# An attention and two feed-forward layers on one core: k loaded ahead of q, and the first sequence's v scaled with its second group of blocks

## Chip, core and metric

The kernel runs on one core of a Trainium2 chip. The metric is device time in microseconds (us) for one whole execution. Three runs of the kernel before gave 715.36, 717.83 and 713.94 us; their median is 715.36 us. The engines are named as the profile names them: PE multiplies matrices, PEld loads its weights, DVE and ACT work on vectors, POOL does small setup work and indirect transfers, SP issues most transfers ("SPq" in a row is its queue of issues).

## What is computed

```
scores = where(block_i >= block_j, q @ k.T / 8, -1e9)     # 4 x 8 heads, 576 rows of 64, blocks of 64
attn   = exp(scores - rowmax); attn /= rowsum + 1e-9
x      = attn @ v                                          # 2304 tokens x 512
x      = elu(x @ w_in) @ w_out                             # 512 -> 2048 -> 512
# then, for tokens with x @ w_skip > 0: the best of 8 experts
e      = argmax(x @ w_gate);  x += gate * (relu(x @ w1[e]) @ w2[e])
```

All of it must come out in f32 accuracy. Much of the kernel therefore multiplies f16 pairs (a high half and the rest, "halves"), and halves need a scale that is found from the size of the data.

## The kernel before

**Attention.** The work is cut into units (sequence b, pair of heads p, block i of 64 queries). A sequence has nine blocks in groups: blocks 0 to 3, then 4 to 7 (with 8 apart in the first sequence). A unit is a score product `s` (PE), a row maximum `mx` (DVE), `e = exp` with its row sum `su` (ACT), the division into `en` or `ehl` (ACT, and DVE for the low half), a transpose into `et`, and, for a whole group, the product `xps` with v (PE), copied into `xt` (ACT). The first sequence is special: q and k come as f32 in a layout that needs no transpose. Blocks 0 to 3 (the first group, needed by the first 256 tokens) use v in f32 straight from the load (`vx`) and `en` in f32, turned on PE (`tp`) and copied to `et` on ACT or DVE. Only its second group uses v's halves (`vt`, made in `prep_v`), which need v's scale: `vflat` loads all of v of one sequence, `vmax` squares and sums it on ACT (the tile `vflat`), and `vscale` brings the sum to all partitions with two small matmuls (`bm1`, `bm2`, tile `bm`) and some DVE steps on `col`.

**First layer.** It goes through nine chunks of 256 tokens. For each, eight products `h = xt @ w_in` of 256 hidden units each, ELU into `g`, and eight products `y += g @ w_out`. The first two chunks use the weights in f32 (`twi`, `two`). The weights arrive as 64-bit values (`rw`), and DVE makes f32 of each half tile with one TENSOR_SCALAR and two SCALAR_TENSOR_TENSOR steps (`conv`, 32 pieces). `h` has two PSUM buffers, `y` two (shared with `bm` and other small products), `s` three. `post` reads `y` into `pay`.

**What sets the order.** Nothing is issued while the program is described. A recorder keeps each step with the tiles it reads and writes, a cost, and its number in the description. `order()` then fills the engines in simulated time: among the steps that are ready on an engine, the one with the lowest number goes first. The description order is thus a priority, and a step that is described later gives way to others. Steps of one engine run strictly in the order so found. The description is given by `A`, `pre`, `post_` and `ex`, lists by position: position x holds the scores of unit x, exponentials of unit x - 1, and so on. `addex(x, ...)` appends steps to position x. The first sequence's first group is positions 0 to 15 and its second group begins at position 16. The first chunk's `h` is described after position 20. SP's transfers are issued one after another, and a transfer that must wait holds up those behind it. Steps in `hot` and the loads at the start have a base of -300, ahead of all others.

**Lines that the change touches.** `load_q0` (two transfers a block, one for each half of the partitions; PE takes it as loaded), `load_k0` (one transfer a block; `prep_k` then scales it by 1/8 on ACT before PE may use it), the `addex` list over b, and the start of the description behind `VF`. All recorded steps have line 320 in the profile, so tiles name them.

Of the kernel before, what the change touches and what calls it, by code (L numbers as in the profile page):

```python
# [357 lines left out]
def tile_kernel(ctx, tc, q, k, v, w_in, w_out, w_skip, w_gate, w1, w2, q0, k0, out):  # L358
# [43 lines left out]
    def newcol(n=1):  # L402
        c = ncol[0]
        ncol[0] += n
        return slice(c, c + n)

    def cf(s):
        return col[:, s]
# [7 lines left out]
    def bc_max(src):  # L416
        p1 = misc([1, 128], "bm1")
        rc.tensor.transpose(out=p1, in_=src, identity=ident)
        t1 = sm.tile([1, 1], BF16, tag="bmt", bufs=2, name="bmt")
        rc.vector.tensor_reduce(out=t1, in_=p1, axis=AX.X, op=ALU.max)  # L420
        p2 = misc([128, 1], "bm2")
        rc.tensor.matmul(out=p2, lhsT=ones16[0:1, :], rhs=t1, start=True, stop=True)
        return p2
# [112 lines left out]
    def scale_bits(T_, S_, I_):  # L536

        Ti = T_.bitcast(I32)
        rc.vector.tensor_scalar(out=Ti, in0=Ti, scalar1=24, scalar2=None, op0=ALU.logical_shift_right)
        rc.vector.tensor_scalar(out=S_.bitcast(I32), in0=Ti, scalar1=-B23, scalar2=204 * B23, op0=ALU.mult, op1=ALU.add)  # L540
        rc.vector.tensor_scalar(out=I_.bitcast(I32), in0=Ti, scalar1=B23, scalar2=50 * B23, op0=ALU.mult, op1=ALU.add)
# [78 lines left out]
    def vflat(b):  # L620
        t = ap.tile([128, H * S * D // 128], F32, tag="kt1", bufs=1, name="vflat")
        rc.sync.dma_start(out=t, in_=v[b].rearrange("s h d -> (s h d)").rearrange("(p x) -> p x", p=128))
        st["vf", b] = t

    def vmax(b):
        if "vmx" not in st:
            st["vmx"] = newcol(4)
        s = st["vmx"].start
        t = st.pop(("vf", b))
        rc.scalar.activation(out=t, in_=t, func=AF.Square, accum_out=col[:, s + b:s + b + 1])  # L630

    def vscale(i):
        s = st["vmx"].start
        if i == 0:
            src = col[:, s:s + 1]
        else:
            c = newcol()
            rc.vector.tensor_reduce(out=cf(c), in_=col[:, s:s + B], axis=AX.X, op=ALU.max)
            src = cf(c)
        T_, S_, I_, P_ = (cf(newcol()) for _ in range(4))  # L640
        rc.vector.tensor_copy(T_, bc_max(src))
        scale_bits(T_, S_, I_)
        rc.vector.tensor_scalar(out=P_, in0=I_, scalar1=2.0 ** 14, scalar2=None, op0=ALU.mult)
        st["v", i] = S_, P_
        if i == 0:
            c = cf(newcol())
            rc.vector.tensor_scalar(out=c, in0=st["v", 0][1], scalar1=2.0 ** -28, scalar2=None, op0=ALU.mult)
            st["x0"] = c
        if i == 1:
            c = cf(newcol())  # L650
            rc.vector.tensor_tensor(out=c, in0=st["v", 0][1], in1=st["v", 1][0], op=ALU.mult)
            c2 = cf(newcol())
            rc.vector.tensor_scalar(out=c2, in0=c, scalar1=2.0 ** -28, scalar2=None, op0=ALU.mult)
            st["mix"] = c2
# [6 lines left out]
    def trows(n):  # L661
        return 128 if n < 4 else 64

    def load_raw(nm, b, n):
        if b == 0 and nm != "v":
            (load_q0 if nm == "q" else load_k0)(n)
            return
        src = {"q": q, "k": k, "v": v}[nm]
        r = trows(n)
        t = ap.tile([128, H, D], F32, tag="raw", bufs=5, name="raw")  # L670
        rc.sync.dma_start(out=t[0:r], in_=src[b, n * 128:n * 128 + r])
        RAW[nm, b, n] = t
# [17 lines left out]
    def load_q0(n):  # L690

        r = trows(n)
        x = QT[0, n] = ap.tile([128, 2, 4, r], F32, tag="qt" if n < 4 else "qh", bufs=3 if n < 4 else 1, name="qx")
        for h in range(2):
            (rc.gpsimd if n > 1 else nc.vector).memset(x[64 - 64 * h:128 - 64 * h, h], 0.0)
        for h in range(2):
            rows = slice(64 * h, 64 * h + 64)
            rc.sync.dma_start(out=x[rows, h].rearrange("p a t -> p (a t)"), in_=q0[rows, 512 * n:512 * n + 4 * r])

    def k0_of(n):  # L700
        return KT[0][:, 512 * n:512 * n + 4 * trows(n)]

    def load_k0(n):

        if n == 0:
            KT[0] = ap.tile([128, 4 * S], F32, tag="kt0", bufs=1, name="kx")
        rc.sync.dma_start(out=k0_of(n), in_=k0[:, 512 * n:512 * n + 4 * trows(n)])

    def load_v0():

        x = X0["v"] = ap.tile([128, 2, H, D], F32, tag="ehl", bufs=2, name="vx")
        for n in range(2):
            rc.sync.dma_start(out=x[:, n].rearrange("p h d -> p (h d)"), in_=v[0, 128 * n:128 * n + 128].rearrange("p h d -> p (h d)"))
            RAW["v", 0, n] = x[:, n]
# [552 lines left out]
    ex = [[] for _ in A]  # L1267

    def addex(x, *fns):
        ex[x].extend(fns)  # L1270

    def L(nm, b, n):
        return lambda: load_raw(nm, b, n)

    def P(f, b, n):
        return lambda: f(b, n)

    for b in range(B):
        g0, g1 = ubase[b, 0], ubase[b, 1]
        if b:  # L1280
            addex(g0 + 1, L("v", b, 1))
        addex(g0 + 1, L("k", b, 2), L("q", b, 2))
        if b:
            addex(g0 + 5, P(prep_v, b, 1))
        addex(g0 + 4, P(prep_k, b, 2), P(prep_q, b, 2), L("v", b, 2), L("k", b, 4))
        addex(g0 + 7, P(prep_v, b, 2), P(prep_k, b, 4), L("q", b, 4), L("v", b, 4))
        addex(g0 + 10, P(prep_q, b, 4), P(prep_v, b, 4), L("k", b, 3), L("v", b, 3), L("q", b, 3))
        addex(g0 + 13, P(prep_k, b, 3), P(prep_v, b, 3))
        addex(g0 + 14, P(prep_q, b, 3))
        if b + 1 < B:  # L1290
            addex(g1 + 8, L("k", b + 1, 0), L("q", b + 1, 0))
            addex(g1 + 11, P(prep_k, b + 1, 0), P(prep_q, b + 1, 0), L("v", b + 1, 0), L("k", b + 1, 1))
            addex(g1 + 14, P(prep_v, b + 1, 0), P(prep_k, b + 1, 1), L("q", b + 1, 1))
            addex(g1 + 18, P(prep_q, b + 1, 1))
# [67 lines left out]

    VF = [4, 5, 6, 6, 7, 8, 9]
    rc.base = -300
    load_q0(0)
    load_k0(0)
    load_q0(1)
    load_k0(1)
    load_v0()
    setup_consts()  # L1370
    for x0, x1, y in ((0, 64, -2048.0), (64, 128, 0.0), (128, 192, 4096.0)):
# [3 lines left out]
    rc.base = 0  # L1375
    load_to(8)
    vflat(0)
    ex[6][0:0] = [lambda: vmax(0), lambda: vscale(0)]
    addex(9, P(prep_v, 0, 0), P(prep_v, 0, 1))
    for x in range(6):  # L1380
        on_a(4 + 2 * x, conv_step)
    for x in range(8):
# [636 lines left out]
```

## Time and profile before

| | us |
|---|---|
| median of three runs | 715.36 |
| lowest, highest | 713.94, 717.83 |
| profiled execution, its own time | 716.24 |
| its span (first to last instruction) | 714.5 |
| PE busy | 678.7 (95%) |
| DVE busy | 568.6 (80%) |
| ACT busy | 504.5 (71%) |
| mean granted PE clock | 0.983 |

The profiled execution's own time has 1.7 us outside its span, and it is 0.88 us above the median. PE is the busiest engine; in the page's 40 slices it is at 9 tenths or more nearly everywhere except the first three slices and the last two. A busy PE can still run at half its clock, which the page gives by slice.

### The profile page before, as it was taken

To read this page: it belongs to the slowest core of one execution; us is meant where nothing else is said; L and a number is where in the kernel's file an instruction comes from. 1 tells how busy PE (TensorE), PEld (TensorE's weight loads), DVE (VectorE), ACT (ScalarE), POOL (GpSimd) and SP (SyncE) were. 2 spreads that over 40 slices of the span, in tenths; PEclk is the share of its full clock that TensorE was granted. 3 is DMA by queue.
4 is the path that set the end of the run, shared out by engine and by line. 5 is a ranking of instruction groups with operands and counts; after the bars stand their busy time and mean duration, and the time that the engine had idled before them with its cause. 6 is when DMAs were issued, how large, how long until landed. Compare 5 with 4: busy or idle time off the path is not lost. (4 is left out here: it accounts for less than half of the span.)

```text
span 714.5 us, 17462 instructions
## 1 busy us (share of the span) xinstructions
PE 678.7 (95%) x6553; PEld 464.8 (65%) x6553; DVE 568.6 (80%) x1640; ACT 504.5 (71%) x1081; POOL 81.9 (11%) x124
## 2 busy tenths in 40 slices
PE   6799998999999999999999999999999999999894
PEld 4478445774576666667656658667576777687683
DVE  5899978988999989988779946999687645666452
ACT  5866478999886878878578736865466548697582
POOL 2000000020001000100100100100105034313012
PEclk9799999999999999999999999999999999999897
DMA  8989999974978788998278159536264779989531
GB/s 281 331 283 377 255 217 202 168 171 88 193 159 137 161 185 216 188 191 176 59 120 176 21 101 337 224 97 200 60 218 132 208 180 240 198 267 207 171 120 17
DMA packets 205882, 130.96 MB, mean 183 GB/s; under 512 B 170699, under 2 KB 171861, under 8 KB 205264
## 3 DMA queue, kind: packets, MB, share of 16 engines
q1 hardware_dynamic: 200736, 120.84, 67.2%
q0 software_dynamic: 3952, 6.70, 4.8%
q10 hardware_dynamic: 1088, 2.10, 0.9%
q8 instruction: 56, 0.92, 0.5%
q14 instruction: 50, 0.41, 0.2%
HBM read 73.59 MB, written 12.75 MB: 121 GB/s over the span
## 5 line engine op out<-in xcount | busy, mean ns | idle before, releaser
L320 PE MATMUL h<-xt,win 128*128 128x256 f16 x1344 | 157.5, 273 | 1.5 <-DVE n L320 1.0
L320 PE MATMUL y<-wout,g 128*128 128x512 f16 x672 | 155.7, 379 | 0.0
L320 PEld LDWEIGHTS <-win 128*128 128x128 f16 x1344 | 128.9, 98 | 23.4 <-issue 1.3
L320 PEld LDWEIGHTS <-g 128*128 128x128 f16 x672 | 63.9, 98 | 66.7 <-issue 0.4
L320 ACT ACTIVATE e<-s,mx 128x512 f32<-128x512 f32 (+4 forms) x160 | 82.1, 516 | 19.6 <-DVE ehl L320 9.2
L320 DVE TENSOR_REDUCE mx<-s 128x1 f32<-128x512 f32 (+4 forms) x160 | 75.3, 477 | 16.6 <-PE s L320 16.0
L320 ACT ACTIVATE ehl<-e,su 128x512 f16<-128x512 f32 (+4 forms) x144 | 74.1, 561 | 12.9 <-DMA et<-ehl 4.0
L320 DVE SCALAR_TENSOR_TENSOR ehl<-e,su,ehl 128x512 f16<-128x512 f32 (+4 forms) x144 | 75.8, 552 | 6.0 <-ACT ehl L320 5.8
L320 PE MATMUL y<-two,g 128*128 128x512 f32 x128 | 59.9, 604 | 0.0
L320 PE MATMUL h<-xt,twi 128*128 128x256 f32 x256 | 59.2, 384 | 0.3 <-DVE g L320 0.3
L320 ACT ACTIVATE g<-el,col 128x512 f16<-128x512 f32 x56 | 40.2, 718 | 21.6 <-DVE el L320 21.3
L320 ACT ACTIVATE el<-h,col 128x512 f32<-128x512 f32 x56 | 38.2, 682 | 24.1 <-PE h L320 22.8
L320 PEld LDWEIGHTS <-p 128*128 128x128 f16 x984 | 46.8, 99 | 9.1 <-PEq L1853 4.1
L320 PEld LDWEIGHTS h<-xt,twi 128*128 128x128 f32 x256 | 47.3, 190 | 7.9 <-issue 1.0
L320 PEld LDWEIGHTS <-vt 128*64 128x64 f16 x1368 | 35.4, 111 | 22.8 <-issue 15.7
L320 PE MATMUL s<-kt,qt 128*64 128x512 f16 (+5 forms) x288 | 48.7, 298 | 0.7 <-ACT e L320 0.5
L320 PE MATMUL xps<-et,vt 128*64 128x128 f16 (+1 forms) x1368 | 44.1, 213 | 3.9 <-DMA et<-ehl 2.2
L320 DVE SCALAR_TENSOR_TENSOR g<-el,col,g 128x512 f16<-128x512 f32 x56 | 41.7, 745 | 3.3 <-ACT g L320 3.0
L320 DVE SCALAR_TENSOR_TENSOR el<-h,col,el 128x512 f32<-128x512 f32 x56 | 41.8, 746 | 1.4
L1554 DVE SCALAR_TENSOR_TENSOR p<-p,n,p 128x1024 f16<-128x1024 f32 x32 | 40.6, 1281 | 2.7 <-ACT p L1553 2.6
L320 PE MATMUL s<-kx,qx 128*128 128x128 f32 (+5 forms) x96 | 34.7, 523 | 7.6 <-ACT kx L320 6.7
L320 POOL DMA_INDIRECT lst_d<-li,si x16 | 19.3, 1209 | 188.5 <-DVE li L320 90.6
(237 smaller groups left out, 1161.7 us busy)
## 6 DMA issues: line engine op xcount, KB each, us to landing
p<-in_moe_w_dram SPq DMA_DIRECT2D x45, 512.0 KB, 5.7
rw<-in_moe_w_in_dram SPq DMA_DIRECT2D x16, 512.0 KB, 8.4
rw<-in_moe_w_out_dram SPq DMA_DIRECT2D x16, 512.0 KB, 7.9
pb<-in_moe_w_dram SPq DMA_DIRECT2D x10, 512.0 KB, 4.9
vflat<-in_v_dram SPq DMA_DIRECT2D x4, 1152.0 KB, 8.9
out_dram<-pay SPq DMA_DIRECT2D x18, 256.0 KB, 3.3
pay_d<-pay SPq DMA_DIRECT2D x18, 256.0 KB, 3.7
raw<-in_v_dram SPq DMA_DIRECT2D x14, 256.0 KB, 3.0
```

The source lines that it names most:

```text
L320: rec.call(e, time, lambda: getattr(self.real, op)(*args, **kw), reads, writes, dma)
L1554: rc.call("dve", 1.2, lambda: nc.vector.scalar_tensor_tensor(out=half(1), in0=raw.t, scalar=sc, in1=half(0), op0=ALU.mult, op1=ALU.subtrac ...
```

## The change

The description changes in two ways, for the first sequence only. At the start, for each of the first two blocks of 128 rows, the transfer of k is issued before the two of q. And v's largest value (`vmax`), its scale (`vscale`) and the five `prep_v` are described at positions 14 to 18, where they stood at positions 6 to 13.

```diff
-        addex(g0 + 7, P(prep_v, b, 2), P(prep_k, b, 4), L("q", b, 4), L("v", b, 4))
-        addex(g0 + 10, P(prep_q, b, 4), P(prep_v, b, 4), L("k", b, 3), L("v", b, 3), L("q", b, 3))
-        addex(g0 + 13, P(prep_k, b, 3), P(prep_v, b, 3))
+        addex(g0 + (7 if b else 17), P(prep_v, b, 2))
+        addex(g0 + 7, P(prep_k, b, 4), L("q", b, 4), L("v", b, 4))
+        addex(g0 + (10 if b else 18), P(prep_v, b, 4))
+        addex(g0 + 10, P(prep_q, b, 4), L("k", b, 3), L("v", b, 3), L("q", b, 3))
+        addex(g0 + 13, P(prep_k, b, 3))
+        addex(g0 + (13 if b else 18), P(prep_v, b, 3))
...
-    load_q0(0)
-    load_k0(0)
-    load_q0(1)
-    load_k0(1)
+    for n in range(2):
+        load_k0(n)
+        load_q0(n)
...
-    ex[6][0:0] = [lambda: vmax(0), lambda: vscale(0)]
-    addex(9, P(prep_v, 0, 0), P(prep_v, 0, 1))
+    addex(14, lambda: vmax(0))
+    addex(15, lambda: vscale(0))
+    addex(16, P(prep_v, 0, 0), P(prep_v, 0, 1))
```

The recorder makes a new order from this. The engines' orders differ from the start through the first three sequences' attention and agree word for word from about 357 us of the trace before to the end. Three places follow.

DVE ahead of the first `h`, before. `mx` are row maxima of the second group's scores, `bmt` is a step of v's scale, `twi` is weight conversion, and `et_263` is the last transposed block that the first chunk needs.

```order
L320 TENSOR_REDUCE mx_255<-s_256 128x1
L320 TENSOR_REDUCE bmt_188<-bm1_187 1x1
L320 SCALAR_TENSOR_TENSOR twi4_280<-rw_146,twi4_280 128x512
L320 TENSOR_SCALAR twi4_280<-rw_147 128x512
L320 COPY et_263<-tp_264 128x512
```

The same place now; `et_261` is the tile that was `et_263`.

```order
L320 TENSOR_REDUCE mx_252<-s_253 128x1
L320 SCALAR_TENSOR_TENSOR twi3_277<-rw_153,twi3_277 128x512
L320 COPY et_261<-tp_262 128x512
L320 SCALAR_TENSOR_TENSOR twi3_277<-rw_153,twi3_277 128x512
L320 TENSOR_REDUCE bmt_242<-bm1_241 1x1
```

The copy of `et` has moved ahead of the scale's `bmt`, with one conversion step ahead of it where two were. On PE the scale's second product `bm2` now stands behind the last product with `et` and ahead of the score product that precedes `h`, and the two score products `s_245` and `s_253` stand next to each other, where a product `xps` stood between them.

SP around the first transposing transfer of the second group, before.

```order
L320 DMA rw_152<-in_moe_w_in_dram 128x2x512
L320 DMA rw_153<-in_moe_w_in_dram 128x2x512
L320 DMA rw_143<-in_moe_w_out_dram 128x1024
L320 DMA_TRANSPOSE et_273<-ehl_267 128x12x128
L320 DMA rw_147<-in_moe_w_out_dram 128x1024
```

The same place now.

```order
L320 DMA rw_152<-in_moe_w_in_dram 128x2x512
L320 DMA_TRANSPOSE et_273<-ehl_267 128x12x128
L320 DMA rw_153<-in_moe_w_in_dram 128x2x512
L320 DMA rw_143<-in_moe_w_out_dram 128x1024
L320 DMA rw_147<-in_moe_w_out_dram 128x1024
```

The transpose, which waits for DVE's `ehl_267`, has moved ahead of the last load of `w_in` and the first of `w_out`.

ACT at the end of the first chunk, before. `pay_413` and `pay_416` are the chunk's two halves read out of PSUM.

```order
L320 ACTIVATE pay_413<-y_302 128x512
L320 ACTIVATE e32_408,su_407<-s_397,mx_396 128x512
L320 ACTIVATE ehl_406<-e32_401,su_400 128x4x128
L320 ACTIVATE ehl_406<-e32_402,su_400 128x64
L320 ACTIVATE e32_409,su_407<-s_398,mx_396 128x64
L320 ACTIVATE pay_413<-pay_413,rts_414 128x512
L320 ACTIVATE pay_416<-y_303 128x512
```

The same place now.

```order
L320 ACTIVATE pay_413<-y_302 128x512
L320 ACTIVATE e32_402,su_400<-s_391,mx_389 128x64
L320 ACTIVATE sq_418,col_77<-twi7_289 128x1024
L320 ACTIVATE pay_416<-y_303 128x512
L320 ACTIVATE ehl_406<-e32_401,su_400 128x4x128
```

The second readout has moved ahead of the attention's steps.

## Rows read from the trace of the kernel before

**Rows 1.** Engines by stretch: us, busy us (instructions), granted PE clock, DMA share, GB/s.

```profile
0.00:38.10 38.10, 26.44 (x132) 16.64 (x132) 27.19 (x86) 25.24 (x73) 6.59 (x44) 0.87 0.95 303
38.10:100.00 61.90, 61.90 (x275) 40.09 (x273) 59.04 (x124) 37.91 (x71) 0.00 (x0) 1.00 0.94 293
100.00:357.00 257.00, 250.51 (x2467) 165.63 (x2466) 230.06 (x742) 212.41 (x527) 15.37 (x23) 1.00 0.82 165
```

**Rows 2.** Timeline of PE around the first h: start, length, engine, step, [idle before <-releaser].

```profile
30.44 1.62 PE L320 MATMUL s<-kx,qx 128*128 128x384 f32 x2 [0.43 <-issue]
...
32.04 0.70 PE L320 MATMUL xps<-et,vx 128*64 128x128 f32 x4
32.67 1.65 PE L320 MATMUL s<-kx,qx 128*128 128x384 f32 x2
...
36.73 0.66 PE L320 MATMUL xps<-et,vx 128*64 128x128 f32 x8 [1.37 <-DVE et L320]
37.32 0.91 PE L320 MATMUL s<-kx,qx 128*128 128x384 f32 x2
...
38.10 5.43 PE L320 MATMUL h<-xt,twi 128*128 128x256 f32 x24
...
47.70 20.97 PE L320 MATMUL h<-xt,twi 128*128 128x256 f32 x96
```

**Rows 3.** Timeline of the start: SP's issues, ACT's scaling of k, PE.

```profile
0.81 1.22 SPq L320 DMA_DIRECT2D qx<-in_q_dram  x2
...
2.08 0.59 SPq L320 DMA_DIRECT2D kx<-in_k_dram  x1
...
5.51 0.63 ACT L320 ACTIVATE kx<-kx 128x512 f32<-128x512 f32 x1 [3.42 <-DMA kx<-in_k_dram]
...
6.19 0.79 PE L320 MATMUL s<-kx,qx 128*128 128x128 f32 x2 [6.19 <-ACT kx L320]
...
7.52 0.63 ACT L320 ACTIVATE kx<-kx 128x512 f32<-128x512 f32 x1 [1.38 <-DMA kx<-in_k_dram]
```

**Rows 4.** Tile qx up to 45 us: from issue to landing of its ten transfers.

```profile
DMA to landing us min/median/max: 3.4/3.7/10.8
```

**Rows 5.** Timeline of DVE ahead of the first h.

```profile
34.40 0.56 DVE L320 TENSOR_REDUCE mx<-s 128x1 f32<-128x384 f32 x1 [1.10 <-PE s L320]
34.88 0.27 DVE L320 TENSOR_REDUCE bmt<-bm 1x1 bf16<-1x128 f32 x1
35.07 0.67 DVE L320 SCALAR_TENSOR_TENSOR twi<-rw,twi 128x512 int32<-128x512 int32 x1
35.67 0.41 DVE L320 TENSOR_SCALAR twi<-rw 128x512 int32<-128x512 int32 x1
36.01 0.67 DVE L320 COPY et<-tp 128x512 f32<-128x512 f32 x1
```

**Rows 6.** Timeline of ACT: the square of the first sequence's v.

```profile
30.24 2.12 ACT L320 ACTIVATE vflat<-vflat 128x2304 f32<-128x2304 f32 x1
```

**Rows 7.** Timeline of ACT, PE and DVE at the first chunk's end.

```profile
115.04 0.58 ACT L320 ACTIVATE pay<-y 128x512 f32<-128x512 f32 x1
...
115.67 0.16 PE L320 MATMUL bm<-bmt,ones 1*128 1x1 bf16 x1 [1.44 <-ACT pay L320]
...
116.11 0.66 DVE L320 TENSOR_REDUCE rts<-pay 128x1 f32<-128x512 f32 x1
```

**Rows 8.** Engines in two stretches ahead of the first h; columns as in rows 1.

```profile
24.60:28.00 3.40, 1.83 (x18) 1.03 (x16) 3.14 (x9) 2.55 (x7) 0.00 (x0) 1.00 1.06 320
28.00:35.20 7.20, 6.51 (x25) 3.54 (x26) 5.47 (x14) 7.01 (x17) 0.36 (x1) 0.53 1.06 305
```

**Rows 9.** Timeline of SP's transpose, and DVE's last piece of w_in.

```profile
44.82 1.57 SPq L320 DMA_TRANSPOSE et<-ehl  x1
...
54.01 0.42 DVE L320 TENSOR_SCALAR twi<-rw 128x512 int32<-128x512 int32 x1
```

**Rows 10.** Tile rw up to 45 us: from issue to landing of its 17 transfers.

```profile
DMA to landing us min/median/max: 7.2/8.4/10.6
```

## The prediction

> **What bounds the kernel now.** I read the table of engines by stretch first. From 38.1 us, where the first `h` product starts, to 100 us PE is busy for all 61.90 us; from 100 to 357 us it is busy for 250.51 of 257 [rows 1]. Before 38.1 us it is busy for 26.44, part of that at half clock: the mean granted clock there is 0.87 [rows 1]. So PE bounds all but the start, and the start is bound by a chain of small steps on four engines that ends when `xt` is complete and `h` can begin. Work that leaves that chain brings `h` forward, and the rest of the program follows, as long as PE stays fed. PE has the same products to do ahead of `h` as before (three score products of the second group among them), so what counts is the moment at which `h` begins, and any new wait after it.
>
> The timeline of PE around that moment comes next [rows 2]: a 1.37 us wait for DVE's `et`, then the last `xps`, one score product, and `h` at 38.10. The timeline of DVE says why `et` was late: after the row maximum at 34.40 come `bmt` (0.27), two conversion steps, and only at 36.01 the copy [rows 5]. At the other end of the chain PE first starts at 6.19 us, on ACT's scaled k [rows 3].
>
> **The change part by part.** Term A, k ahead of q. No instruction is added; the same three issues a block change places. PE needs scaled k and raw q. Before, SP issues q's two transfers from 0.81 on (1.22 us) and k at 2.08; k has landed by 5.51, ACT scales it for 0.63, and PE starts at 6.19 [rows 3]. Now k goes at 0.81 and, at the shortest landing of such a transfer, 3.4 us [rows 4], is scaled by 0.81 + 3.4 + 0.7 = 4.9, and the last of q is issued at about 0.81 + 0.59 + 0.61 = 2.0, which lands between 5.4 (3.4 us) and 5.7 (3.7 us) [rows 4]. So q ends the wait in place of k and the 0.63 us of scaling no longer stands behind the last landing: PE starts at about 5.5, a gain of 0.7. If PE needs only q's first half for its first product, which lands some 0.6 earlier, the gain is 1.1. The second block goes the same way: k has landed by 7.52 and is then scaled for 0.63 [rows 3], and now the last of q lands when k did. That is the same 0.7 and not a second one. Weight loads behind these issues leave when they left before, and DVE's conversions start no earlier; where such a step takes DVE at a bad moment the gain can go down to 0. I take 0.7, between 0 and 1.1.
>
> The Trainium skill, "DMA: Bandwidth & Descriptors", section "Anatomy of one DMA — SWDGE (gpsimd) path", gives about 2.0 us plus size over 436 GB/s for a transfer, 2.6 us for k's 256 KB as an estimate. The shortest landing of these transfers here is 3.4 us [rows 4], so the trace does not agree; by the page q would land about 1.1 us sooner and term A would be 1.8.
>
> Term B, v's scale behind the first group's last steps. Nothing is added or removed: the square of v (2.12 us on ACT [rows 6]), the two small products and the `col` steps are all still done ahead of the first `h` or beside it, and the five `vt` stay behind `h`'s start as before. What moves is the order within the chain. First, the two score products now stand next to each other. Before, `xps` stood between them, and the second began at 32.67 where the product with `xps` had begun at 32.04 [rows 2]: 0.63 earlier. Second, DVE now does one fused step between the row maximum and the copy of `et`. Before it was 36.01 - 34.40 = 1.61 from the one to the other; now it is the maximum's 0.48 (34.88 - 34.40) and the step's 0.60 (35.67 - 35.07), 1.08 in all [rows 5]: 0.53 earlier. Third, a new wait: PE's `bm2` now stands between the last `xps` and the last score product, and needs `bmt`, which DVE does behind the copy and one more fused step. From the copy's start that is 0.60 + 0.60 + 0.27 and some 0.15 for the hand-overs, about 1.65, where it was 37.32 - 36.01 = 1.31 before [rows 2, 5]: 0.34 later. Queued behind `bm2` on PE are the score product and `h` itself, so this counts in full. Sum: 0.63 + 0.53 - 0.34 = 0.8.
>
> The square itself now follows the last `en` on ACT. Its cover is PE's two score products, 3.3 us [rows 2], while it takes 2.12 plus a readout, so I cost it at nothing; if it began only with the second of them, 2.12 - 1.65 = 0.5 us of it would show in front of `bm2`, and B would be 0.3. Upward, B reaches 2.3 if PE has its full clock there: the score product took 1.62 and 1.65 us at a granted clock of 0.53 and 0.91 at full clock [rows 2, 8], 1.45 us less for the two. I take 0.8, which goes by the rows next to it.
>
> Term C, the end of the first chunk. PE waited 1.44 us for ACT to read `y` out at 115.04 [rows 7]. ACT now does that readout ahead of four attention steps, so this wait goes. What is late next: `bm2` of the second router scale waits for DVE, which now has the maximum over `pay` (0.66 [rows 7]) and some `rts` steps in front of it. I take that new wait at the maximum's 0.66 and some 0.3 for the small steps, so 0.5 is left. Bounds: 1.44 if no wait follows, -0.6 if the maximum comes on top of the old wait.
>
> Term D, all other reordering up to 357 us. PE's idle time between 100 and 357 us is 257 - 250.51 = 6.49 us [rows 1], 1.44 of it counted in C. At most 5.05 can go, and nothing excludes as much on the other side. I take 0. Behind 357 us the orders are the same, and everything moves as a whole.
>
> Sum: 0.7 + 0.8 + 0.5 = 2.0 us. The profiled execution took 716.24, so its like now would take 714.2. It is 0.88 above the median of 715.36; the median now is 713.4 us.
>
> **The rivals.** Rival 1, PE keeps its full clock. Between 28 and 35.2 us the granted clock is 0.53, nearly all of it at the 1.2 GHz level, and in the 3.40 us before it fell PE had been busy for only 1.83, at 1.00 [rows 8]; from 38.1 us, with PE busy all the time, it is 1.00, the 2.4 GHz level [rows 1]. If fewer waits stand ahead of it, the two score products save 1.45 us: 713.4 - 1.45 = 712.0. Against it: the wait of the second `xps` for ACT stays, since ACT has as much to do in front of it. The Trainium skill, "TensorE: Matmul & The Clock Gate", section "HAM oscillation — how this bites in real kernels", says that waits between short groups of products make the clock fall again and again. By that rule this rival gets its time if the waits shorten; the trace agrees that the clock falls behind a stretch with waits.
>
> Rival 2, DVE becomes the bound behind `h`. It was busy for 59.04 of the 61.90 us after 38.1 [rows 1]. An `h` chunk takes PE 20.97 / 6 = 3.5 us [rows 2], and in the new order DVE has four fused steps, two TENSOR_SCALAR and one step on `g` per chunk: 5 x 0.60 + 2 x 0.34 = 3.7 by the spacing of [rows 5]. `h` has two PSUM buffers and waits for `g` two chunks back. If DVE has no lead, about 0.2 a chunk is lost over six chunks, 1.2 us, and if C does not come either the time is 715.4 - 2.0 + 1.2 + 0.5 = 715.1, no change.
>
> Rival 3, slower: the transpose holds up weight loads. It waits for DVE's `ehl`, went out at 44.82 and took 1.57 of SP [rows 9]. The last load of `w_in` stands behind it now and leaves at about 44.82 - 1.5 + 1.57 = 44.9. It lands at 53.3 at the median of 8.4 us, at 55.5 at the longest of 10.6 [rows 10]. DVE reached this piece at 54.01 [rows 9] and would now at 52.5, with `g` behind it, so DVE waits 0.8 to 3.0 us; PE has about 1 us of slack there (an estimate from the order's steps and rows 5). At 10.6 us the 2.0 us gain is used up; from about 11 us of landing on, the kernel is slower, and at 13 us it takes 715.4 - 2.0 + (3.0 + 2.4 - 1.0) = 717.8. For it: the loads share the engines, whose share is 0.94 here [rows 1]. Against: no load in that stretch took more than 10.6.
>
> Rival 4, the reordering up to 357 us gains 2 us or more of its 5.05: 711.4 or less. With the other sign it is slower, 715.4 or more.
>
> **How the numbers follow.** About 0.5% (3.6 us) is what a measurement of this kernel tells from no change: under 711.8 is faster, over 718.9 slower. Chances: the forecast (711.8 to 714.6) 0.45, rival 1 0.15, rival 2 0.20, rival 3 0.08, rival 4 0.12 (0.07 down, 0.05 up). Faster gets half of rival 1, nearly all of rival 4's lower side and 0.11 of the forecast for D and for the noise of the median (the three runs lie 3.9 us apart): 0.25. Slower gets half of rival 3, 0.03 of rival 4's upper side and 0.03 for noise: 0.10. Same: 0.65. The range leaves 1 in 10 on either side: downward, 713.4 less 1.45 for the clock, 0.9 for C and 1.6 of D, 709.5; upward, rival 3 at a landing of just under 13 us, 717.3.
>
> **What would show it.** A: PE's first product at 5.1 to 5.7 us, waiting for `qx`, not for ACT. B: `h` begins at 36.6 (38.10 - 0.7 - 0.8), with `bm2` waiting for DVE in front of it; at 35.2 or less with a granted clock near 1 it is rival 1. C: the wait of 1.44 us at 115 is gone and a shorter one for DVE's `bmt` follows. Rival 2 shows as PE waiting for `g` between 45 and 62 us, rival 3 as DVE waiting for `rw` there. The forecast is wrong if `h` does not begin earlier, or if it does and the first chunk's end does not.

## The result and the profile after

The changed kernel takes 719.28 us at the median of 11 runs (717.78 to 722.24), the kernel before on the same chip 715.36 (710.82 to 718.11, 11 runs). The ratio is 1.0057, with a 95% interval of 1.0034 to 1.008: slower by some 0.6%, or 4 us. The profiled execution took 721.03 us. The ratios leave out executions over 1.5% above the fastest of their kernel; the medians of the tables keep them.

The table of engines by stretch answers to [rows 1]; its columns are the same.

```profile
0.00:38.10 38.10, 28.33 (x161) 19.42 (x162) 31.35 (x97) 30.10 (x83) 6.59 (x44) 1.00 0.96 307
38.10:100.00 61.90, 61.90 (x304) 37.60 (x303) 57.92 (x119) 36.18 (x70) 0.00 (x0) 1.00 1.05 307
100.00:357.00 257.00, 242.46 (x2383) 161.04 (x2379) 225.18 (x732) 208.65 (x517) 13.80 (x23) 0.99 0.83 161
```

The reader is to see two things. The front is better than forecast: its granted clock is 1.00 where it was 0.87. And between 100 and 357 us PE is now idle for 257 - 242.46 = 14.54 us, where it was idle for 6.49.

The start, which answers to [rows 3] (timeline of SP's issues, ACT and PE):

```profile
0.81 0.39 SPq L320 DMA_DIRECT2D kx<-in_k_dram  x1
...
1.25 1.20 SPq L320 DMA_DIRECT2D qx<-in_q_dram  x2
...
3.70 0.63 ACT L320 ACTIVATE kx<-kx 128x512 f32<-128x512 f32 x1 [1.61 <-DMA kx<-in_k_dram]
...
4.41 0.77 PE L320 MATMUL s<-kx,qx 128*128 128x128 f32 x2 [4.41 <-ACT kx L320]
```

And PE around the first `h`, which answers to [rows 2]:

```profile
29.51 0.27 PE L320 MATMUL bm<-ident,col 128*1 128x128 f32 x1 [0.62 <-ACT vflat L320]
30.04 0.66 PE L320 MATMUL xps<-et,vx 128*64 128x128 f32 x8 [0.26 <-DVE et L320]
...
30.91 0.91 PE L320 MATMUL s<-kx,qx 128*128 128x384 f32 x2
...
31.69 7.15 PE L320 MATMUL h<-xt,twi 128*128 128x256 f32 x32
```

PE starts 1.78 us sooner, and `h` 6.4 us sooner than in the profile before. All of that is lost again, and 4.7 us more, behind 100 us. PE's timeline from 100 to 245 us, its rows with the longer waits, the two `h` rows behind 115 us and a later one:

```profile
103.65 0.86 PE L320 MATMUL xps<-et,vt 128*64 128x128 f16 x24 [1.52 <-DMA et<-ehl]
...
110.17 0.34 PE L320 MATMUL s<-kx,qx 128*64 128x64 f32 x4 [1.24 <-ACT e L320]
...
114.25 0.16 PE L320 MATMUL bm<-bmt,ones 1*128 1x1 bf16 x1 [1.10 <-DVE bmt L320]
115.12 0.34 PE L320 MATMUL s<-kx,qx 128*64 128x64 f32 x4 [0.72 <-ACT e L320]
115.39 2.68 PE L320 MATMUL h<-xt,twi 128*128 128x256 f32 x8
...
118.12 2.86 PE L320 MATMUL h<-xt,twi 128*128 128x256 f32 x8
...
142.75 1.97 PE L320 MATMUL h<-xt,twi 128*128 128x256 f32 x8
...
188.62 0.66 PE L320 MATMUL xps<-et,vt 128*64 128x64 f16 x30 [0.73 <-DMA et<-ehl]
...
208.21 0.66 PE L320 MATMUL xps<-et,vt 128*64 128x64 f16 x30 [1.14 <-DMA et<-ehl]
...
226.24 0.66 PE L320 MATMUL xps<-et,vt 128*64 128x64 f16 x30 [1.13 <-DMA et<-ehl]
```

Grouped by what ended them, the waits of that stretch are, in the changed kernel (us in total, times, longest):

```profile
PE xps L320 <- DMA et<-ehl: 6.0, 5, 1.5
PE s L320 <- ACT e L320: 2.8, 4, 1.2
PE bm L320 <- DVE bmt L320: 1.1, 1, 1.1
PE lp L320 <- DMA x2t<-pay: 1.0, 2, 0.5
```

and in the kernel before:

```profile
PE bm L320 <- ACT pay L320: 1.4, 1, 1.4
PE s L320 <- ACT e L320: 0.5, 1, 0.5
PE h L320 <- DVE el L320: 0.5, 1, 0.5
PE h L320 <- DVE g L320: 0.3, 1, 0.3
PE xps L320 <- DMA et<-ehl: 0.3, 1, 0.3
```

So PE is now ready for the attention's products with v before their transposed `et` has landed, and for the scores before ACT has read the old ones (`s` waits for `e`). Behind the waits of 110 to 115 us the clock falls too (windows, columns as in rows 1):

```profile
109.50:114.00 4.50, 2.98 (x52) 1.89 (x53) 4.29 (x29) 4.33 (x10) 0.20 (x1) 1.00 0.90 207
114.00:115.50 1.50, 0.54 (x6) 0.31 (x6) 1.50 (x8) 1.50 (x6) 0.00 (x0) 1.00 0.94 346
115.50:120.00 4.50, 4.50 (x16) 3.55 (x17) 4.17 (x22) 4.04 (x13) 0.20 (x1) 0.62 0.86 184
```

At 0.62 for 4.5 us some 1.7 us of work are lost (4.5 x 0.38); the 8 products of an `h` take 2.68 and 2.86 us there, 1.97 at full clock. The sum for the two profiles: PE's idle time from 100 to 450 us is 7.33 us before and 16.39 after, 9.1 more; with 1.7 for the clock and 6.4 gained in front that is 4.4 us, and the spans differ by 4.7.

### The profile page after: what moved, and what is told of

Read it like the earlier page. It is cut to its first block, busy times and chain, and to the rows that moved or that the text cites. A ratio compares the mean times of both kernels' runs of the same rounds, so it can differ in the third digit from the quotient of the medians.

```text
span 719.2 us, 17484 instructions
## 1 busy us (share of the span) xinstructions
PE 675.4 (94%) x6553; PEld 462.0 (64%) x6553; DVE 567.9 (79%) x1640; ACT 504.7 (70%) x1081; POOL 81.0 (11%) x124
## 5 line engine op out<-in xcount | busy, mean ns | idle before, releaser
L320 PE MATMUL h<-xt,twi 128*128 128x256 f32 x256 | 61.0, 391 | 0.0
L320 PE MATMUL xps<-et,vt 128*64 128x128 f16 (+1 forms) x1368 | 44.2, 213 | 11.1 <-DMA et<-ehl 8.2
L320 PE MATMUL s<-kt,qt 128*128 128x512 f16 (+5 forms) x288 | 49.1, 299 | 1.1 <-ACT e L320 0.9
L320 PEld LDWEIGHTS <-hh 128*64 128x64 f16 (+1 forms) x432 | 28.7, 106 | 17.3 <-DVE hh L320 2.1
```

The costliest lines, as they stand in the source:

```text
L320: rec.call(e, time, lambda: getattr(self.real, op)(*args, **kw), reads, writes, dma)
```

## The experiments

Twelve kernels ran in three groups of four, in the order of the table; each ratio is against the kernel before on the same chip. That took 716.76 us on the chip of the first group, 715.97 on the second and 718.8 on the third, so medians do not compare between groups. The ratio is not the quotient of two medians (for new_to_h that is 0.997), and a difference between two rows is to be read with both intervals. Where a row has line 327 for 320, the kernel has seven lines more ahead of it. "Idle" is PE's idle time from 100 to 450 us in the profiled execution, from a row by stretch; "first h" is from PE's timeline, with the granted clock up to 38.1 us.

| kernel | ratio (95%) | median us | idle us | first h (clock) |
|---|---|---|---|---|
| before | 1 | 715.36 to 718.8 | 7.3 | 38.10 (0.87) |
| changed | 1.0057 (1.0034 to 1.008) | 719.28 | 16.4 | 31.69 (1.00) |
| k_first | 1.0052 (1.0023 to 1.0081) | 719.92 | 14.6 | 32.14 (1.00) |
| v_late | 1.0004 (0.9969 to 1.0038) | 716.97 | 9.7 | 35.18 (1.00) |
| old_order_k_first | 0.9962 (0.9931 to 0.9993) | 712.3 | 8.4 | 33.78 (1.00) |
| new_order_q_first | 1.0074 (1.0049 to 1.0099) | 721.5 | 14.9 | 35.91 (0.91) |
| new_to_h | 1.0002 (0.9973 to 1.0032) | 714.14 | 10.0 | 34.28 (0.91) |
| new_to_chunk1 | 0.9977 (0.9952 to 1.0002) | 715.28 | 11.2 | 33.35 (0.96) |
| new_to_chunk2 | 1.0027 (1.0 to 1.0055) | 717.69 | 13.7 | 34.53 (0.96) |
| late_et_k_first | 1.003 (1.0005 to 1.0055) | 717.88 | 9.8 | 32.09 (1.00) |
| old_to_chunk1 | 1.0087 (1.0053 to 1.0121) | 725.1 | 16.3 | 36.51 (0.85) |
| lat_pe25 | 1.0015 (0.9978 to 1.0052) | 719.92 | 10.8 | 36.35 (0.91) |
| lat_pe22 | 0.9974 (0.9935 to 1.0014) | 718.18 | 10.1 | 36.05 (0.91) |
| lat_act26 | 1.0033 (0.9987 to 1.008) | 724.0 | 10.9 | 35.22 (0.87) |

**Which half of the change, and is it the transfers or the order?** The first four runs. The first two make one half of the change alone: k_first has only the new places of the loads of k and q, v_late only the new positions of `vmax`, `vscale` and the five `prep_v`.

> Only k ahead of q; vmax, vscale and prep_v described where they were before. The order that the recorder makes from this is the changed kernel's, but for a swap of two neighbours on ACT and on DVE. Theory O (the loss sits in the new order from 100 to 245 us, and the k swap alone makes that order): 719 us, h begins at 31 to 32.5, PE waits about 11 us between 100 and 245 us. Theory V (the moved v steps cause the loss): 712 to 715 us, about 3 us of waits there.

> Only the v steps described later; q ahead of k as before. PE's and SP's orders are those of the kernel before, word for word. Theory O: no change, 715.4 us within 1, h begins at 38, about 3.3 us of PE's waits between 100 and 245 us. Theory V: about 719 us with about 11 us of waits there.

The halves are cleanly apart. With k first alone the kernel is the changed one (1.0052, idle 14.6, of it 9.0 from 100 to 245 us, where 11 were expected); with the v steps alone it is the one before (1.0004). The moved v steps change the places of a few neighbouring `vt` steps on ACT and DVE, and nothing on PE or SP. Theory V falls. The run with the v steps gives a second reading as well: with PE's order of before, but at full clock in front, its `h` begins at 35.18.

```profile
0.00:38.10 38.10, 24.91 (x145) 16.38 (x146) 29.60 (x95) 26.98 (x77) 6.61 (x44) 1.00 0.95 303
```

So up to 2.9 of the 6.4 us between the two profiles go with the clock in front, which can be full with PE's order of before too (0.3 of it is there at PE's first product already, 5.92 against 6.19). Whether the change makes that more frequent is open: over all executions the mean granted clock was 0.987 for the kernel before on this chip, 0.989 for v_late and new_order_q_first, and 0.991 for k_first and old_order_k_first (the changed kernel: 0.992). Without the 2.9 us the two profiles would differ by 7.6, where the medians differ by 4, so some of it may be typical of the change.

Then the two things that the swap of k and q does were taken apart: the transfers themselves, and the order that the recorder makes. The order was made first, and the six issues (`first` in the code) changed places afterwards.

```diff
-        for i in self.order():
+        seq = self.order()
+        if self.first:
+            at = sorted(seq.index(i) for i in self.first)
+            for x, i in zip(at, self.first):
+                seq[x] = i
...
+        for i in seq:
```

> The order of the kernel before on every engine; only when it is issued do the six transfers of q and k for the first two blocks change places on SP, so that k leaves first. Theory O: h begins 1.8 us or more earlier (34 to 36.3), the waits between 100 and 245 us stay at 3 to 4 us, and the gain lasts to the end: 711.5 to 714 us. Theory G (whatever begins earlier is given back there, since transposes, ACT and DVE supply PE no sooner): the waits grow by what h gained, to 5 us or more, and the time is 715 to 716 us.

> The changed kernel's order on every engine; only the same six transfers change places back when issued, so that q leaves first. Theory O: h begins 1 to 2 us later than in the changed kernel (33 to 34), the waits between 100 and 245 us stay at about 11 us: 720 to 722 us. Theory G: the waits shrink by what h loses, to 9 us or less, and the time is 719.3 us or less.

In the old order with k first, PE starts at 4.47 us and `h` at 33.78, 1.40 ahead of the 35.18 of v_late (both at full clock, PE's order the same):

```profile
4.47 0.80 PE L327 MATMUL s<-kx,qx 128*128 128x128 f32 x2 [4.47 <-ACT kx L327]
...
33.78 5.43 PE L327 MATMUL h<-xt,twi 128*128 128x256 f32 x24
```

v_late:

```profile
5.92 0.80 PE L320 MATMUL s<-kx,qx 128*128 128x128 f32 x2 [5.92 <-ACT kx L320]
...
35.18 5.43 PE L320 MATMUL h<-xt,twi 128*128 128x256 f32 x24
```

From 100 to 450 us (columns as in rows 1; the first line is old_order_k_first):

```profile
100.00:450.00 350.00, 341.62 (x3412) 227.10 (x3407) 301.07 (x965) 271.49 (x654) 18.68 (x29) 1.00 0.77 164
```

v_late:

```profile
100.00:450.00 350.00, 340.33 (x3402) 226.09 (x3401) 299.56 (x954) 270.75 (x654) 18.17 (x29) 1.00 0.78 162
```

The waits did not grow (8.38 against 9.67), and the gain lasts to the end: the span is 708.1 against 710.5. Theory G falls on this. The other run is less clear. Its time is the one of theory O (721.5 us, 1.0074, where G had 719.3 or less), but its waits from 100 to 245 us are 8.5 us, under the 9 of theory G; the changed kernel has 11.1 there and k_first 9.0. From 100 to 450 us they are 14.9, 16.4 and 14.6. Its `h`, expected at 33 to 34, begins at 35.91, with a clock of 0.91 in front. With the order held, k ahead of q gains about 0.4% (0.07 to 0.69); the new order costs more than that, 0.9% between old_order_k_first and k_first, which have the same transfers and ran on the same chip.

**Where in the order?** The recorder's steps are the same in both orders, so a kernel can follow one order up to a planned time (`CUT`) and the other behind it. All four have k first. The time is one of the order that comes first (100.3 us of the new plan, 101.9 of the old one at the first readout), so old_to_chunk1 is nearly, and not exactly, the complement of new_to_chunk1.

```diff
+    start = {i: steps[i][6] for i in new}
+    front = [i for i in new if start[i] < CUT]
+    seq = front + [i for i in old if start[i] >= CUT]
```

> k first. The new order up to the first h, and the order of the kernel before for all that is left. Theory L (each stretch's own order causes the waits in it): h begins at 31.5 to 32.5 us as in the changed kernel, the waits between 100 and 245 us are the 3 to 4 us of the old order, and the time is 709 to 711.5 us, under the 712.3 of the old order with k first. Theory E (PE that comes 2 us sooner outruns its suppliers there): waits of 5 us or more, 712 us or more.

> k first. The new order to just ahead of the first readout of y (about 106 us), the old order from there. Theory L: it holds the wait of 1.5 us for a transpose at 103 us, but not those that follow: waits of 4 to 6 us between 100 and 245 us, 711 to 713 us. If the loss were made by what the stretch up to 106 us leaves undone (theory U), the waits behind it would come all the same: 9 us or more, 717 us or more.

> k first. The new order to just ahead of chunk 1's first readout (about 190 us), the old order from there. Theory L: it holds the waits from 103 to 138 us and the stretch of half clock at 115 to 120 us (some 5.5 us in all against the old order), not the 4.4 us of waits behind 180 us: 714 to 717 us, and PE's waits from 180 to 245 us are 1 to 2 us. Theory U: they are 4 us or more, and the time is 719 us or more.

> k first. The order of the kernel before to just ahead of the first readout of y (about 106 us), the new order from there: the complement of the cut at chunk 1. If the parts of the loss add up (theory L), what the cut at chunk 1 did not hold is here: 712.3 + 719.9 - 715.3 = 716.9 us, with half clock again at 115 to 120 us. If the loss needs the new front (theory E), 713 us or less.

As ratios against old_order_k_first (0.9962), the new order up to the first readout adds 0.15%, up to the second one 0.65%, and all of it 0.9%; each of these is good to some 0.4%, so the first is not told from nothing. The old order up to the first readout and the new one behind it add 1.25%, about 9 us, and that kernel's interval lies clear of new_to_chunk1's. So the loss sits in the new order behind 106 us. The waits agree: old_to_chunk1 is idle for 16.3 us, 7.9 more than old_order_k_first, and new_to_chunk2 has 2.2 us of waits from 180 to 245 us, a little over the 1 to 2 expected, where k_first has 4.1. Theory U falls (new_to_chunk1: 5.2 us of waits where it asked for 9, 715.28 us where it asked for 717). Theory E falls on old_to_chunk1, which has the old front and yet 725.1 us where it asked for 713 or less.

Theory L's times were missed in all four. new_to_h was to be faster than old_order_k_first, at 709 to 711.5 us; it took 714.14 (1.0002), and the intervals of the two overlap. It has the waits of theory L, 3.9 us, but its `h` came at 34.28 and not at 31.5 to 32.5, with a clock of 0.91 in front. It follows SP's old order word for word, yet waits 1.57 us at 105.78 for a transpose. new_to_chunk1 has the waits expected of it (5.2 us in the two stretches from 100 to 145 and 180 to 245 us), but 715.28 us where 711 to 713 were expected; new_to_chunk2 has 717.69 for 714 to 717. old_to_chunk1 was to take 716.9 us and to show half clock at 115 to 120 us; it took 725.1, on the slowest of the three chips, and has no fall of the clock from 100 to 145 us (1.00). The two cuts at 106 us come to 1.4% where the whole has 0.9%; with some 0.6% of uncertainty in that difference (an estimate from the four intervals), the runs do not show that the parts fail to add up. A cut order is also a third order, at its seam above all.

**Is the recorder's model at fault, or is it any new order?** Last, the costs in the recorder were changed, with k first.

```diff
late_et_k_first, transposes count as landing 1.0 us later:
-    lat = ... else self.LAT[e]
+    lat = ... else self.LAT[e] + (e == "sp" and s[1] >= 1.2)
lat_pe25, lat_pe22 ("pe": 0.25, 0.22), lat_act26 ("act": 0.26):
-    LAT = {"pe": 0.2, "dve": 0.23, "act": 0.23, ...}
+    LAT = {"pe": 0.25, "dve": 0.23, "act": 0.23, ...}
```

> k first, a new order throughout: the recorder now counts a transposing transfer as landing 1.0 us later than it did (it put 3.7 us from issue to use; the trace of the changed kernel has 4.1 us to landing at the median). Theory M (the waits come since the recorder takes transposes as done too soon): PE's waits for et between 100 and 300 us fall from 8 us to 3 or less, 710 to 713 us. Theory C (any new order is a new draw, with its waits at other places): the waits for et shrink, but others of 3 us or more take their place, 715 to 721 us.

> k first. The recorder counts 0.25 us from PE to the next engine where it counted 0.20; nothing else is changed, and it makes another order. Its own plan leaves PE idle for 1.2 us between 95 and 350 us (3.5 in the plan of the order before, 4.6 in that of the changed kernel). Theory P (what the plan leaves idle is what the chip waits, plus a part common to all): 708 to 711 us. Theory C (any new order is a new draw): anywhere from 711 to 720 us, whatever the plan says.

> k first. As the run with 0.25 us, with 0.22 us: a third order; its own plan leaves PE idle for 2.6 us between 95 and 350 us. Theory P: 710.5 to 712 us. Theory C: anywhere from 711 to 720 us.

> k first. The recorder counts 0.26 us from ACT to the next engine where it counted 0.23: a fourth order; its own plan leaves PE idle for 2.0 us between 95 and 350 us. Theory P: 709.5 to 711.5 us. Theory C: anywhere from 711 to 720 us.

PE's waits of late_et_k_first from 100 to 300 us:

```profile
PE s L320 <- ACT e L320: 2.8, 3, 1.2
PE xps L320 <- DVE col L320: 1.3, 1, 1.3
PE xps L320 <- DMA et<-ehl: 0.8, 3, 0.3
PE xps L320 <- DVE xt L320: 0.7, 1, 0.7
```

Its partner is k_first, which has 4.5 us of waits for `et` and 4.6 of others in the same stretch. (The 8 us of the expectation are the changed kernel's up to 450 us; up to 300 us it has 6.0.) So the waits for `et` fell by 3.7 us to 0.8, as theory M had it, and the others rose by 0.8 to 5.4; PE's idle time up to 450 us fell from 14.6 to 9.8. The time fell far less, to 1.003, for the clock took much of it: in late_et_k_first it falls from 112 us on.

```profile
112.00:120.00 8.00, 6.08 (x73) 4.71 (x70) 7.35 (x35) 8.00 (x21) 0.43 (x2) 0.58 0.97 210
```

At 0.58 for 8 us that is 3.4 us of work, where k_first lost 1.6 in the same way (0.65 from 115.5 to 120 us). Counted against the kernel before, 2.5 us more of idle time and 3.4 for the clock give back nearly all of the 6.0 us by which `h` came sooner, and the span is 715.5 against 714.5. From 100 to 145 us the mean clock is 0.92 to 0.96 in every kernel with a new order over the whole program, and 1.00 with the old one.

The other three runs speak against theory P: the order whose own plan has the least idle time (1.2 us, lat_pe25) is 1.0015, the one with 2.0 us is 1.0033, and the one with 2.6 us is 0.9974. The first two lie outside the times of theory P; lat_pe22 by itself would not exclude them. Theory C gave times that little could refute (711 to 720 or 721 us); three of the four runs lie within them, and lat_act26, with 724.0 us on the slowest chip, only by its ratio. The other half of theory C, that waits of 3 us or more come elsewhere in late_et_k_first, is not what its trace shows. With k first, six orders over the whole program were measured: the old one 0.9962, the others 0.9974, 1.0015, 1.003, 1.0033 and 1.0052. The old one is the lowest; lat_pe22 cannot be told from it.

## Why the prediction was wrong

The step that failed is term D, "all other reordering up to 357 us", taken at 0 with bounds of 5.05 us on either side, and term C as its first piece. PE's idle time from 100 to 357 us rose from 6.49 to 14.54, by 8.05 us, and the clock's fall cost 1.7 more; without term C's 1.6 (below) this is 8.1 us for D, against a bound of 5.05. What made it is the new order that the swap of k and q brings (k_first against old_order_k_first). The bounds were a mistake of their own: idle time before limits what can be gained, and nothing limits the loss. The upper bound was set equal to the lower one for want of a reason, and it turned out to be too small.

**Term A** (k ahead of q, 0.7, at most 1.1) was too small: PE's first product came 1.45 us sooner at equal order and clock (5.92 in v_late, 4.47 in old_order_k_first). In the changed kernel the first transfer landed 2.9 us after its issue (0.81 to 3.70, the hand-over included) where the prediction took 3.4, and q, which was to end PE's wait, did not: PE still waited for ACT's `kx`. The estimate from the Trainium skill in the prediction, "DMA: Bandwidth & Descriptors", "Anatomy of one DMA — SWDGE (gpsimd) path", 1.8 us for this term, was nearer than mine, though the section's fit is for transfers that GpSimd issues and these are SP's. At the first `h`, 1.40 of the gain was left.

**Term B** (0.8, between 0.3 and 2.3) came out at twice its size, within its bounds, and by another cause; that it lies within them is luck. The new order brings `h` forward by a further 1.6 to 2.1 us at full clock (33.78 to 32.14 and 31.69). But the v steps, to which I gave it, do nothing to PE's order: the swap of k and q makes all of it. Had each half of the change been planned by itself, this could have been seen before any run. The wait for the square, set at 0.5 at most in front of `bm2`, came at 0.62 in front of the first `bm` (for `vflat`); `bm2` itself did not wait.

**Term C** (0.5, from -0.6 to 1.44): the 1.44 us wait went, as forecast, and a wait of 1.10 for `bmt` came near the 0.96 forecast, but not by the forecast's reason. The maximum over `pay` had run on DVE at 108.64 us, long before; what stood right ahead of that `bmt` (113.92) was an `ehl` step of the attention (0.74). What I left out were the two score products that wait for ACT's `e` (1.24 and 0.72 us). Ahead of the first of these `e` (109.33) ACT now does the second readout (108.00); how much of the 1.24 us that makes was not separated. Together 3.06 us stand for 1.44: -1.6, beyond the lower bound.

**The rivals.** Rival 1 looks right in the profile after (clock 1.00, score products of 0.88 and 0.89 us), but v_late shows the same clock with PE's order of before, so the profile does not prove it. Whether the change makes the full clock more frequent is open; the mean clocks above leave room for it. Rivals 2 and 3 did not come: PE was busy for all 61.90 us behind 38.1, though the transpose stood ahead of the weights on SP. Rival 4 with the other sign is what happened, at 5% and with no price beyond "715.4 or more".

What stays open: why PE's products and the transposes miss each other in the new order was not taken apart further. Whether PE is early or a transpose late differs from wait to wait. For the wait of 1.52 us at 103.65 it is the transpose that is late: it was issued at 97.4 us, and the same one at 97.5 us in old_order_k_first, but it landed 1.7 us later (rows below).

## What to carry to other kernels

Where a planner sets the order, a change of two transfers is two changes, the transfers and a new order for everything; plan each edit by itself to see which of them moves the order, and price the transfers with the old order held. A new order is to be measured against the old one: here five new orders all came out at or above it, and the plan with the least idle time was not the fastest. Idle time before bounds the gain, not the loss. A gain in idle time is to be read together with the clock. If only the physical effect is wanted, move the transfer and keep the order.

## What the runs showed of the hardware

**The spread goes with the clock.** In 65 executions of the kernel before (the first two groups of runs) the mean granted clock lay between 0.978 and 0.996, and a straight line through them has 4.9 us less for each 0.01 more; the times between 711.0 and 720.5 us. In front it shows in two profiles: the stretch up to 38.1 us had 0.87 in the profile before and 1.00 in v_late with PE's order the same, and `h` began 2.9 us apart. A difference in front between two single profiles is therefore read only with the clock beside it.

**The same transpose lands in 4.5 or in 6.2 us.** The `et` issued at about 97.5 us, in old_order_k_first (times in us):

```profile
L327 SPq DMA_TRANSPOSE et<-ehl x1: 1605/1605/1605, 97.5 to 97.5; - x1
...
DMA to landing us min/median/max: 4.5/4.5/4.5
```

and in the changed kernel:

```profile
L320 SPq DMA_TRANSPOSE et<-ehl x1: 1462/1462/1462, 97.4 to 97.4; - x1
...
DMA to landing us min/median/max: 6.2/6.2/6.2
```

It took 4.4 in the profiles of the kernel before and of v_late, and 6.0 to 6.3 in those of k_first, new_order_q_first, new_to_h, new_to_chunk1 and new_to_chunk2. So the short time goes with the old order up to the first `h`, 60 us sooner, and the long one with the new order there: new_to_h has only that much of the new order, and SP's order is the old one throughout. Before the transpose lands in new_to_h, at 105.8 us, the DMA engines moved 6 GB/s for a microsecond (last column):

```profile
103.00:104.00 1.00, 1.00 (x3) 0.19 (x1) 0.79 (x3) 1.00 (x5) 0.00 (x0) 1.00 1.96 190
104.00:105.00 1.00, 0.21 (x1) 0.11 (x1) 0.33 (x2) 1.00 (x3) 0.00 (x0) 1.00 1.02 6
105.00:106.00 1.00, 0.22 (x8) 0.22 (x9) 0.00 (x0) 0.23 (x2) 0.00 (x0) 1.00 0.69 162
```

In the changed kernel the microsecond from 102 to 103 us has 4 GB/s. The DMA share (the column ahead of it) does not tell whether the engines were busy: it is 1.96 in the first row here, which is more than a whole, and 0.04 in the slow microsecond of the changed kernel. What the engines do in it, and why this transpose and not its neighbour meets it, no run here shows.
